# Scale and epsilon of the pooled softmax on ScalarE, and a weight queue that runs fourteen blocks ahead

## The chip, the cores and the metric

The kernel runs on one core of a Trainium2 chip. The metric is the device time of one execution in microseconds (us). Engines: PE (TensorE), DVE (VectorE), ACT (ScalarE), POOL (GpSimd) and SP, which here only issues DMAs, in order.

## What is computed

The reference, cut to what matters (batch 8, 8 heads, 576 positions, 64 elements a head):

```python
q_d, k_d, v_d = means over groups of 4 positions          # 144 pooled positions
s = scale * q_d @ k_d.T;  s = s - max(s);  a = exp(s);  a = a / (sum(a) + 1e-9)
out_up = repeat(a @ v_d, 4)
s = where(|i - j| < 4, scale * q @ k.T, -1e9)              # local attention
out_local = softmax(s, with the same 1e-9) @ v
x = (out_up + out_local) as 4608 rows of 512
h = x @ w_in                                               # 512 -> 2048
out = (h * clip(h + 3, 0, 6) / 6) @ w_out                  # 2048 -> 512
```

## The kernel before, in words

**Attention units.** A unit is one batch and a pair of heads: 8 x 4 = 32 units. Each has local scores (L570) and pooled scores (L399 or L413), two softmaxes, and the products with V (L610 local, L533 or L544 pooled). For the pooled scores, three columns of 144 in PSUM, DVE takes the maximum (L437, `top`), DVE multiplies it by -1/128 (L428, `down`), ACT does three exponentials with that as bias and with the sum as second output (L433, `weigh`), POOL adds 1e-9 to the three sums (L449, `plus`), DVE takes the reciprocal (L452) and DVE or POOL multiplies (L455, `norm`). The first two batches (8 units) transpose their weights on PE (`alone`, L464 and L593, copied out of PSUM by L119 on ACT or L121 on DVE); the other 24 units send them through DRAM and back (L477, L485, L490 pooled; L504, L511 local) and transpose on DVE (L499, L518). In those 24 the pooled scores lie in two banks: two columns in one, the third behind local scores in another; `top` and `weigh` are each called twice.

**Matrix products.** After attention the rows go in chunks through GEMM1 (L865, 16 blocks `f` of `w_in`), an activation (L871 on ACT, L875 on DVE, L879 on ACT, L883 on DVE or POOL) and GEMM2 (L915, 16 blocks of `w_out`). Chunk 0 has 512 rows. PE mixes the units of later batches with the GEMMs of the chunk that runs. In GEMM names, `h` is GEMM1's PSUM tile, `o` (and one `a`) those of GEMM2; `a` tiles otherwise belong to attention, and there are three `a` banks.

**Weights.** 32 blocks of 512 KB come as 64-bit words and are converted: L172 or L176 and L190 on ACT, L181 and L185 on DVE, L195 (high part) on ACT, L199 (low part) on DVE or POOL. The block order is i0 to i3, i4, o0, i5, o1, i6, o2, i7, o3, i8, o4 and so on (i of `w_in`, o of `w_out`). The first `GATE` = 10 loads wait only for the first inputs (and, where they use a place that early attention still holds, for that). Block n from 10 on waits until the high part of block n - 10 has been made. Beside this gate, every DMA that SP issues waits for the one eight before it.

**Order.** A planner written in the kernel (`Plan`, with costs given in each `op` call) runs through a model of the five engines and writes the instructions out in the order that comes of it. So a changed cost or dependency shifts the order of everything behind it. Engines then run their own lists in order, held only by semaphores.

## Time and profile before

| | us |
|---|---|
| median of 3 runs | 963.71 (962.75 to 965.15) |
| the profiled execution, own time | 966.26 |
| its span, first to last instruction | 964.5 |
| PE busy | 936.4 |
| DVE, ACT, POOL busy | 591.5, 343.2, 287.9 |

The profile is one execution. Its page gives busy time by engine, the chain of work that ended last, and groups of like instructions by line of the kernel; the trace can be asked for waits, stretches and single instructions. A busy PE is not PE at its peak, since its clock can be granted at half.

### The profile page before, as it was taken

How to read it: one execution, taken by the hardware profiler on the slowest of the kernel's cores; microseconds unless marked ns; L12 is line 12 of the kernel's file. 1: busy time of each engine (PE TensorE's matmuls, PEld its weight loads, DVE VectorE, ACT ScalarE, POOL GpSimd, SP SyncE). 2: the span in 40 equal slices, each digit the busy share in tenths (PEclk: the TensorE clock that was granted, in tenths of full speed). 3: DMA queues.
4: the chain of work that ended last, by engine and by line, in shares of the span. 5: the costliest groups of instructions: out<-in, count | busy, mean ns of one | idle time of the engine just before them, and what ended most of it. 6: DMA issues, size and time to landing. Idle time of an engine off the chain costs nothing.

```text
span 964.5 us, 19717 instructions
## 1 busy us (share of the span) xinstructions
PE 936.4 (97%) x7503; PEld 810.5 (84%) x7503; DVE 591.5 (61%) x1131; ACT 343.2 (36%) x805; POOL 287.9 (30%) x385
## 2 busy tenths in 40 slices
PE   8879998999999999999999999999999999999996
PEld 5558777888889788888988988888988988998995
DVE  7989787577766667657556566646645663223322
ACT  4878652334223223323323322323322322322321
POOL 5842445154535334224123223223303210000000
PEclk9979998999999999999999999999999999999999
DMA  7996525356664563545514554554424420100101
GB/s 215 251 240 210 115 80 101 87 106 128 130 133 101 108 129 76 117 79 109 118 30 83 117 101 96 121 109 80 105 47 98 95 60 1 34 1 1 34 1 33
DMA packets 311374, 93.52 MB, mean 97 GB/s; under 512 B 251376, under 2 KB 297328, under 8 KB 311280
## 3 DMA queue, kind: packets, MB, share of 16 engines
q1 hardware_dynamic: 311280, 92.27, 43.3%
q8 instruction: 59, 0.97, 0.4%
q14 instruction: 35, 0.29, 0.1%
HBM read 69.60 MB, written 22.61 MB: 96 GB/s over the span
## 4 chain that ended last, share of the span: by engine, by line
PE 79%; SPq 6%; DVE 4%; DMA 4%; POOL 3%; issue 2%; ACT 1%; DVEq 0%; POOLq 0%; ACTq 0%
PE h L865 35%; PE o L915 35%; PE a L610 2%; SPq L300 2%; PE a L570 1%; SPq L485 1%; PE a L915 1%; DMA arena<-in_k_dram 1%; PE a L413 1%; SPq L490 1%; PE a L533 1%; DMA rawo<-in_w_out_dram 1%; DMA arena<-pl 1%; DMA arena<-pd 1%; SPq L511 1%
## 5 line engine op out<-in xcount | busy, mean ns | idle before, releaser
L915 PE MATMUL o<-wo,rounded 128*128 128x512 f32 x1680 | 432.0, 398 | 2.7 <-ACT wo L195 1.3
L865 PE MATMUL h<-rounded,wi 128*128 128x384 f32 (+2 forms) x2240 | 432.8, 337 | 0.9 <-DVE arena L875 0.8
L865 PEld LDWEIGHTS h<-rounded,wi 128*128 128x128 f32 x2240 | 390.7, 189 | 23.7 <-issue 1.8
L915 PEld LDWEIGHTS o<-wo,rounded 128*128 128x128 f32 x1680 | 310.4, 189 | 64.0 <-issue 3.8
L875 DVE SCALAR_TENSOR_TENSOR arena<-arena,h 128x384 f32<-128x384 f32 (+2 forms) x192 | 104.3, 544 | 175.0 <-ACT arena L871 174.6
L871 ACT ACTIVATE arena<-h 128x384 f32<-128x384 f32 (+2 forms) x192 | 94.5, 492 | 313.8 <-PE h L865 281.9
L879 ACT CAST rounded<-arena 128x384 fp32r<-128x384 f32 (+2 forms) x192 | 98.4, 513 | 135.8 <-DVE arena L875 96.5
L883 POOL TENSOR_TENSOR rounded<-arena,rounded 128x384 fp32r<-128x384 f32 (+2 forms) x55 | 60.3, 1098 | 250.7 <-PE o L915 118.7
L883 DVE TENSOR_TENSOR rounded<-arena,rounded 128x384 fp32r<-128x384 f32 (+2 forms) x137 | 77.9, 571 | 87.4 <-PE o L915 61.0
L433 ACT ACTIVATE arena<-a,arena 128x144 f32<-128x144 f32 x84 | 31.2, 378 | 94.8 <-DVE arena L428 80.7
L455 POOL TENSOR_TENSOR arena<-arena 128x640 f32<-128x640 f32 (+1 forms) x38 | 41.8, 1111 | 17.1 <-DVE arena L452 15.5
L307 DVE STREAM_TRANSPOSE arena<-arena 128x576 f32<-128x576 f32 x56 | 42.6, 765 | 3.2 <-DMA arena<-in_k_dram 1.9
L366 DVE TENSOR_REDUCE arena<-arena 128x128 f32<-128x512 f32 (+2 forms) x34 | 36.5, 1073 | 4.8 <-PE a L533 4.3
L792 POOL TENSOR_TENSOR rounded<-arena,rounded 128x768 fp32r<-128x768 f32 (+2 forms) x9 | 12.4, 1396 | 86.7 <-DVE rounded L121 86.7
L440 POOL TENSOR_TENSOR arena<-arena 128x640 f32<-128x640 f32 x23 | 29.0, 1262 | 27.9 <-DVE arena L437 16.2
L499 DVE STREAM_TRANSPOSE arena<-arena 128x384 f32<-128x384 f32 (+1 forms) x48 | 22.0, 466 | 24.9 <-DMA arena<-pd 24.4
L518 DVE STREAM_TRANSPOSE arena<-arena 128x640 f32<-128x640 f32 x24 | 20.3, 844 | 21.5 <-DMA arena<-pl 21.4
L449 POOL TENSOR_SCALAR arena<-arena 128x10 f32<-128x10 f32 (+1 forms) x60 | 16.1, 268 | 51.1 <-ACT arena L433 41.5
L610 PEld LDWEIGHTS a<-arena 64*64 64x64 f32 x1140 | 21.0, 137 | 12.1 <-issue 3.6
L320 POOL TENSOR_TENSOR arena<-arena 128x144 f32<-128x144 f32 x24 | 11.1, 463 | 64.6 <-PE a L413 22.8
L570 PE MATMUL a<-arena 64*64 64x64 f32 x1220 | 29.4, 224 | 0.0
L322 POOL TENSOR_TENSOR arena<-arena 128x144 f32<-128x144 f32 x48 | 28.3, 589 | 3.8
(184 smaller groups left out, 836.4 us busy)
## 6 DMA issues: line engine op xcount, KB each, us to landing
rawi<-in_w_in_dram SPq DMA_DIRECT2D x16, 512.0 KB
rawo<-in_w_out_dram SPq DMA_DIRECT2D x16, 512.0 KB
arena<-in_q_dram SPq DMA_DIRECT2D x112, 72.0 KB
arena<-in_k_dram SPq DMA_DIRECT2D x112, 72.0 KB
pl<-arena SPq DMA_DIRECT2D x24, 320.0 KB
arena<-pl SPq DMA_DIRECT2D x96, 80.0 KB
arena<-in_v_dram SPq DMA_DIRECT2D x28, 256.0 KB
out_dram<-arena SPq DMA_DIRECT2D x96, 72.0 KB
```

Source lines behind the costliest of these rows:

```text
L307: nc.vector.transpose(out=qk[kind], in_=st["raw", kind].rearrange("p j i -> p (j i)"))
L366: eng.tensor_reduce(out=vd, in_=raw.rearrange("p r e -> p e r"), op=ALU.add, axis=AX.X)
L433: nc.scalar.activation(p[:, j], x[:, j], AF.Exp, bias=m[:, j:j + 1], scale=1.0 / 128.0, accum_out=s[:, j:j + 1])
L455: eng.tensor_tensor(x, x, s.unsqueeze(2).broadcast_to(list(x.shape)), op=ALU.mult)
L570: nc.tensor.matmul(st["ps", g][half:half + WIN, jj * D:jj * D + WIN], qk_of("q")[hs, k_first:k_first + WIN], qk_of("k")[hs, k_first:k_firs ...
L610: nc.tensor.matmul(st["px"][g][h * D:(h + 1) * D, at + lo:at + hi], st["v"][ks, jj, h * D:(h + 1) * D], st["pt"][ks, jj, half + lo:half + ...
L865: nc.tensor.matmul(st["ps"], win[f][:, wt, kk * P:(kk + 1) * P], xs[part][:, kk], start=(kk == 0 and i == 0), stop=(kk == NK - 1 and i == ...
L871: nc.scalar.activation(st["t"], st["ps"], AF.Relu, bias=3.0)
L875: nc.vector.scalar_tensor_tensor(out=t, in0=t, scalar=6.0, in1=st["ps"], op0=ALU.min, op1=ALU.mult)
L879: nc.scalar.copy(st["gh"], st["t"])
L883: eng.tensor_tensor(st["gl"], st["t"], st["gh"].bitcast(F32), op=ALU.subtract)
L915: nc.tensor.matmul(otile[n, m], gt[:, ms], wout[f][:, wt], start=(f == 0 and i == 0), stop=(f == NF - 1 and i == 2),)
```

## The change

The multiplication by -1/128 (`down`) goes from DVE to ACT, and the addition of 1e-9 to the pooled sums from POOL to ACT; both stand in `weigh`, around the exponentials. In the 24 later units each of the two `weigh` calls now waits for its own maximum only, where both waited for both. The local softmax keeps its POOL addition, with a planner's cost of 0.35 for 0.15. `GATE` goes from 10 to 14. Both versions hold the same matrix products; the changed one has five fewer of the 512-column products (35 to 30) that only keep PE busy before the first GEMM.

```diff
         def down(m):
-            nc.vector.tensor_scalar(m, m, -1.0 / 128.0, None, op0=ALU.mult)
+            nc.scalar.activation(m, m, AF.Copy, scale=-1.0 / 128.0)
 
         def weigh(x, p, m, s):
+            down(m)
             for j in range(x.shape[1]):
                 nc.scalar.activation(
                     p[:, j], x[:, j], AF.Exp, bias=m[:, j:j + 1], scale=1.0 / 128.0, accum_out=s[:, j:j + 1])
+            nc.scalar.activation(s, s, AF.Copy, bias=1e-9)
...
         if alone:
-            def top_d():
-                top(rows_d(), st["md"])
-                down(st["md"])
-
-            a = op("DVE", 0.68, top_d, [sd])
-            sums_d = [op("ACT", 1.74, lambda: weigh(rows_d(), st["pd"], st["md"], st["sd"]), [a], free=[bk])]
+            a = op("DVE", 0.6, lambda: top(rows_d(), st["md"]), [sd])
+            sums_d = [op("ACT", 2.2, lambda: weigh(rows_d(), st["pd"], st["md"], st["sd"]), [a], free=[bk])]
         else:
             def top_d(i):
                 x, _, m, _ = rows_d4(i)
                 top(x, m)
-                if i:
-                    down(st["md"])
 
             a, sums_d = [], []
             for i in range(2):
-                a.append(op("DVE", 0.45 - 0.07 * i, partial(top_d, i), [sd] + a))
+                a.append(op("DVE", 0.45 - 0.15 * i, partial(top_d, i), [sd]))
             for i in range(2):
-                sums_d.append(op("ACT", 1.16 - 0.58 * i, lambda i=i: weigh(*rows_d4(i)), a, free=[(bk, bks[1])[i]]))
-        a = op("POOL", 0.15, lambda: plus(st["sd"]), sums_d)
-        a = op("DVE", 0.18, lambda: recip(st["sd"]), [a])
+                sums_d.append(op("ACT", 1.62 - 0.58 * i, lambda i=i: weigh(*rows_d4(i)), [a[i]], free=[(bk, bks[1])[i]]))
+        a = op("DVE", 0.18, lambda: recip(st["sd"]), sums_d)
...
-        a = op("POOL", 0.15, lambda: plus(st["s"]), [a])
+        a = op("POOL", 0.35, lambda: plus(st["s"]), [a])
...
-PRE, GATE = 4, 10
+PRE, GATE = 4, 14
```

In the changed file lines stand up to five lower or higher; its L860, L866, L870, L874, L878, L910 are the GEMM lines L865, L871, L875, L879, L883, L915 of before, and L439, L586, L520, L629 are L437, L584, L518, L627. The DVE line L428 is an ACT line now.

**The start, SP's list.** Before, ahead of batch 1's second load of queries and keys (L300); `rawi` and `rawo` are weight blocks, here i4, o2, i5, and i6 at the end:

```order
L161 DMA rawi_520<-in_w_in_dram 128x1024
L161 DMA rawo_540<-in_w_out_dram 128x1024
L161 DMA rawi_548<-in_w_in_dram 128x1024
L300 DMA arena<-in_q_dram 32x18x32 x4
L300 DMA arena<-in_k_dram 32x18x32 x4
L340 DMA arena<-in_v_dram 64x4x128
L344 DMA arena<-in_v_dram 64x128
L161 DMA rawi_751<-in_w_in_dram 128x1024
```

And now (579 is o3, 784 is i6, 791 is o4):

```order
L161 DMA rawi_531<-in_w_in_dram 128x1024
L161 DMA rawo_541<-in_w_out_dram 128x1024
L161 DMA rawi_570<-in_w_in_dram 128x1024
L161 DMA rawo_579<-in_w_out_dram 128x1024
L300 DMA arena<-in_q_dram 32x18x32 x4
L340 DMA arena<-in_v_dram 64x4x128
L344 DMA arena<-in_v_dram 64x128
L300 DMA arena<-in_k_dram 32x18x32 x4
L161 DMA rawi_784<-in_w_in_dram 128x1024
L161 DMA rawo_791<-in_w_out_dram 128x1024
```

Block o3 moved ahead of those loads, and o4 behind i6; the keys moved behind the values.

**The same place, ACT's list.** Before, from the wait for i6 (751) to the copy out of PSUM that stood on ACT:

```order
L172 ACTIVATE o_860<-rawi_751 128x512
L871 ACTIVATE arena<-h_834 128x512
L879 CAST rounded<-arena 128x512
L190 ACTIVATE rawi_751<-rawi_751 128x512
L879 CAST rounded<-arena 128x512
L119 COPY arena<-a_879 16x3x2x48
```

Now, from the wait for i6 (784) to the second copy (`a_895`) that the first batch-1 product with pooled V needs:

```order
L172 ACTIVATE o_855<-rawi_784 128x512
L866 ACTIVATE arena<-h_830 128x512
L190 ACTIVATE rawi_784<-rawi_784 128x512
L176 ACTIVATE rawo_791<-rawo_791 128x512
L195 CAST wi_878<-o_811 128x512
L874 CAST rounded<-arena 128x512
L866 ACTIVATE arena<-h_857 128x512
L119 COPY arena<-a_890 128x3x2x48
L195 CAST wi_901<-early 128x512
L119 COPY arena<-a_895 16x3x2x48
```

The one copy on ACT stood five instructions behind the wait, and DVE made the other; now both stand on ACT, the later one nine instructions behind the wait.

**The end of chunk 0, DVE's list.** Before, around the second step (L185) of o14 (`rawo_1520`); `a_1858` and `a_1868` come from one unit's transposes and products with V on PE:

```order
L875 SCALAR_TENSOR_TENSOR arena<-arena,h_1794 128x512
L181 SCALAR_TENSOR_TENSOR arena<-rawo_1520 128x512
L307 STREAM_TRANSPOSE arena<-arena 128x576
L316 TENSOR_REDUCE arena<-arena 128x144
L121 COPY arena<-a_1858 128x256
L185 SCALAR_TENSOR_TENSOR arena<-rawo_1520,arena 128x512
L627 TENSOR_TENSOR arena<-a_1868,arena 128x288
```

And now (o14 is `rawo_1631`, o15 `rawo_1636`; `h_1774` and `h_1867` are GEMM1's last two blocks, f = 14 and 15):

```order
L870 SCALAR_TENSOR_TENSOR arena<-arena,h_1774 128x512
L181 SCALAR_TENSOR_TENSOR arena<-rawo_1631 128x512
L181 SCALAR_TENSOR_TENSOR arena<-rawo_1636 128x512
L185 SCALAR_TENSOR_TENSOR arena<-rawo_1631,arena 128x512
L878 TENSOR_TENSOR rounded<-arena,rounded 128x512
L121 CAST rounded<-arena 128x2x192
L121 CAST rounded<-arena 128x2x64
L870 SCALAR_TENSOR_TENSOR arena<-arena,h_1867 128x512
```

The copy out of PE's transposes no longer stands ahead of o14's second step, and that step moved ahead of the gate of f = 15.

**A unit in the middle, DVE's list.** Before, the eighth of the 24 units (a_3755 to a_3757 are its three banks of scores):

```order
L518 STREAM_TRANSPOSE arena<-arena 128x640
L584 TENSOR_TENSOR arena<-a_3755,mask 128x5x64
L584 TENSOR_TENSOR arena<-a_3756,mask 128x5x64
L437 TENSOR_REDUCE arena<-a_3757 128x2
L437 TENSOR_REDUCE arena<-arena 128x10
L437 TENSOR_REDUCE arena<-a_3756 128x1
L428 TENSOR_SCALAR arena<-arena 128x3
```

And now:

```order
L520 STREAM_TRANSPOSE arena<-arena 128x640
L870 SCALAR_TENSOR_TENSOR arena<-arena,h_3751 128x384
L307 STREAM_TRANSPOSE arena<-arena 128x576
L316 TENSOR_REDUCE arena<-arena 128x144
L586 TENSOR_TENSOR arena<-a_3779,mask 128x5x64
L586 TENSOR_TENSOR arena<-a_3780,mask 128x5x64
L439 TENSOR_REDUCE arena<-a_3781 128x2
L439 TENSOR_REDUCE arena<-arena 128x10
L439 TENSOR_REDUCE arena<-a_3780 128x1
```

The scaling is gone from DVE, and three instructions of other work moved between the transpose and the masks. On PE, the products with V of the unit before stand behind nine GEMM2, twelve GEMM1 and nine GEMM2 products after these scores before, and behind nine and twelve now.

## Rows read from the trace of the kernel before

**Rows 1.** The page's first part: busy us (share) and instructions of an engine.

```profile
PE 936.4 (97%) x7503; PEld 810.5 (84%) x7503; DVE 591.5 (61%) x1131; ACT 343.2 (36%) x805; POOL 287.9 (30%) x385
```

**Rows 2.** Stretches: length, busy of PE, PEld, DVE, ACT, POOL; clock; DMA share; GB/s.

```profile
44.00:68.00 24.00, 16.68 (x193) 11.64 (x187) 21.34 (x40) 19.65 (x43) 13.68 (x17) 0.85 0.86 208
...
156.00:168.00 12.00, 9.55 (x76) 7.80 (x75) 8.28 (x14) 2.06 (x4) 4.68 (x4) 0.72 0.62 123
...
319.00:334.00 15.00, 13.54 (x147) 10.91 (x147) 11.50 (x23) 4.32 (x13) 5.60 (x8) 0.89 0.52 96
334.00:950.00 616.00, 614.95 (x4568) 547.99 (x4567) 336.30 (x637) 183.35 (x430) 136.66 (x179) 1.00 0.35 73
```

**Rows 3.** PE's waits: for whom, us in total, times, longest.

```profile
PE o L915 <- ACT wo L195: 1.3, 1, 1.3
PE o L915 <- POOL wo L199: 0.8, 1, 0.8
```

**Rows 4.** Timeline, PE, 53 to 68 us: start, us, what [idle before].

```profile
53.58 0.39 PE L865 MATMUL h<-rounded,wi 128*128 128x512 f32 x1
...
59.06 1.42 PE L544 MATMUL a<-arena 128*64 128x144 f32 x8 [2.74 <-DVE arena L121]
...
62.12 1.49 PE L610 MATMUL a<-arena 64*64 64x60 f32 x38 [0.38 <-ACT arena L119]
...
67.18 1.06 PE L570 MATMUL a<-arena 64*64 64x64 f32 x40
68.17 0.79 PE L865 MATMUL h<-rounded,wi 128*128 128x512 f32 x1
```

**Rows 5.** Timeline, ACT, 56 to 57 us.

```profile
56.18 0.63 ACT L172 ACTIVATE o<-rawi 128x512 f32<-128x512 f32 x1 [2.70 <-DMA rawi<-in_w_in_dram]
56.74 0.58 ACT L871 ACTIVATE arena<-h 128x512 f32<-128x512 f32 x1
```

**Rows 6.** Timeline, SP, 44 to 51 us: loads as issued.

```profile
44.33 4.96 SPq L300 DMA_DIRECT2D arena<-in_k_dram  x4
...
50.63 0.58 SPq L161 DMA_DIRECT2D rawi<-in_w_in_dram  x1
```

**Rows 7.** The chain that ended last, 157 to 161 us: start, us, what.

```profile
157.17 1.41 DVE arena L185
...
158.60 0.63 ACT wo L195
...
159.29 1.28 POOL wo L199
```

**Rows 8.** Line L428, its instructions: ns least/median/most.

```profile
L428 DVE TENSOR_SCALAR arena<-arena x30: 169/675/1172, 13.4 to 775.7; 128x3 f32<-128x3 f32 x30
```

**Rows 9.** Timeline, POOL, 28 to 31 us.

```profile
28.81 2.11 POOL L455 TENSOR_TENSOR early<-early,arena 128x640 f32<-128x640 f32 x2
```

**Rows 10.** Timeline, DVE, 29 to 31 us.

```profile
29.69 1.26 DVE L428 TENSOR_SCALAR early<-early 128x3 f32<-128x3 f32 x1
```

**Rows 11.** Groups by line: count, busy us, mean ns, idle before.

```profile
L549 ACT ACTIVATE arena<-a 128x144 f32<-128x144 f32 x28 | 8.2, 293 | 11.1 <-PE a L533 9.5 <-PE a L544 1.6
...
L433 ACT ACTIVATION_READ_ACCUMULATOR arena<-a,arena 128x1 f32 x84 | 16.8, 200 | 0.0
```

**Rows 12.** Timeline, PE, 319 to 329 us.

```profile
319.39 0.58 PE L413 MATMUL a<-arena 64*64 64x144 f32 x10
...
328.85 0.74 PE L610 MATMUL a<-arena 64*64 64x57 f32 x34 [1.46 <-ACT arena L433]
```

**Rows 13.** Timeline, DVE, 323 to 328 us.

```profile
325.36 0.44 DVE L437 TENSOR_REDUCE arena<-a 128x2 f32<-128x288 f32 x1
...
326.77 1.11 DVE L428 TENSOR_SCALAR arena<-arena 128x3 f32<-128x3 f32 x1
```

**Rows 14.** Timeline, ACT, 328 us.

```profile
327.96 0.38 ACT L433 ACTIVATE arena<-a,arena 128x144 f32<-128x144 f32 x1 [5.50 <-DVE arena L428]
```

**Rows 15.** The chain that ended last, 397 us: nine products of GEMM2.

```profile
397.25 2.26 PE o L915 x9
```

## Prediction

> **What bounds the kernel now.** I began with the page's first part: PE is busy for 936.4 us of a span of 964.5, DVE for 591.5 [rows 1]. So the time is PE's products, plus about 28 us in which PE stands, plus what a halved clock takes. A change that touches only DVE, ACT and POOL can win or lose at those two places alone. The second view, busy time by stretch, says where they are [rows 2]. From 334 to 950 us PE works 614.95 of 616 us at full clock: nothing is to be won there, only lost. In 44 to 68 PE works 16.68 of 24 us at a mean granted clock of 0.85, in 156 to 168 it works 9.55 of 12 at 0.72, in 319 to 334 it works 13.54 of 15 at 0.89. The clock has two levels (1.2 and 2.4 GHz); a mean of 0.85 over 24 us is 7.2 us at the lower one, which costs half of that, 3.6 us. In the same way the second place costs 3.4 us and the third 1.65. Each time PE had just stood.
>
> The waits of PE, the timelines and the chain of waits tell what it stood for.
>
> *The start.* The third block of GEMM1 ends at 53.58 + 0.39 = 53.97 us, the fourth (f = 3) begins only at 68.17 [rows 4]. Between them stand attention products, of which the first with pooled V waits 2.74 us for a copy by DVE; DVE is busy for 21.34 and ACT for 19.65 of these 24 us. ACT stood 2.70 us for weight block i6, until 56.18 [rows 5]. SP issued that load at 50.63, behind batch 1's keys and values, which it had begun to issue before 44.33 [rows 6].
>
> *The end of chunk 0.* DVE's second step of o14 begins at 157.17 (in the order ahead, a copy of PE's transposes stands ahead of it), then come ACT at 158.60 and POOL at 159.29 [rows 7]. GEMM2 waits 1.3 us for ACT's part and 0.8 for POOL's [rows 3].
>
> *In the middle.* At 327 to 329 us PE waits 1.46 us for exponentials, 328.85 - 319.39 = 9.46 us after it began that unit's pooled scores [rows 12]. The chain there is `top` 325.36, `down` at 326.77, which takes 1.11 us, exponentials at 327.96 [rows 13, 14].
>
> **The change part by part. 1. The scaling leaves DVE.** The 32 instructions L428 take 169 ns at the least, 675 in the median, 1172 at the most [rows 8] (30 on that row and two with another name, as in [rows 10]); 32 x 0.675 = 21.6 us of DVE. The long ones are not arithmetic on 128x3 numbers. One began at 29.69 and ran 1.26 us, to 30.95; POOL's multiplication beside it ended at 28.81 + 2.11 = 30.92 [rows 9, 10]. I read this as DVE held until POOL lets go.
>
> DVE has 279.7 us to spare in 616 (336.30 busy), so from 334 us on these microseconds are off the path: 0. At the start, where DVE is nearly full, eight units pass and the stalls lie on the path; a gain from them is inside the bounds of point 3.
>
> **2. ACT gains 112 small instructions**: two in each of 8 early units, four in each of 24 later ones. The trace has no such copy. The nearest rows are ACT's 128x1 read of an accumulator, 200 ns, and a 128x144 activation, 293 ns [rows 11]. So one costs 0.2 to 0.29 us, and all 22 to 33 us of ACT. ACT is busy for 183.35 of 616 us in the middle [rows 2]; there they lie on no path except the unit's own chain. In that chain `top`, the wait, `down` (1.41 + 1.11 us from 325.36 to 327.88 at the eighth unit, [rows 13]) become `top` (0.44) and one ACT copy (0.2 to 0.29): the first exponentials can start about 1.8 us earlier after the first maximum. POOL's addition goes to ACT as well, which shortens the other side of the chain by a handover; it is not waited for by PE in any row here: 0. At the start 16 of the copies stand in ACT's list, where it is busy 82%: 16 x 0.25 = 4.0 us over all 8 units; if four of them fall ahead of the wait that ends last there, 1 us, which is within the bounds of point 3.
>
> **3. GATE 14, at the start.** o3 now stands ahead of batch 1's loads on SP, and o4 behind i6; 14 blocks are loaded before a conversion is asked for. What is queued behind: SP's queue puts o3's 524 kB ahead of batch 1's keys and i6. At the stretch's 208 GB/s [rows 2] that is 2.5 us, so i6 lands at 56.2 (no change, if the transfers had room) to 58.7; or at 53.5, if its issue goes forward by as much. On ACT both copies that the first batch-1 product with pooled V needs stand behind the wait for i6, the later one behind nine other instructions. ACT's instructions begin 0.56 us apart [rows 5]; with the two smaller copies the ten take, as an estimate, 4.8 us. Then come the L544 and L593 products, 1.4 us at full clock (L544 took 1.42 at half, [rows 4]), and 0.4 for handovers: f = 3 starts 6.6 us after i6 lands. With 56.2 that is 62.8, against 68.17: 5.4 us earlier. But L610 (1.49) and L570 (1.06), which stood ahead of f = 3, now follow it: 2.5 us of the work is only moved. The net is -2.9; with 53.5 it is -5.6, with 58.7 it is -0.4. f = 3's own weight can also be ready only late; its low part is made some 7 us of DVE's work earlier in the new list, so it is not what comes last there. If the nine instructions on ACT take half as long again (2.4 us more) behind a late i6, the sum is +2.0. I take -2.5, nearest to the landing seen, less a little for ACT's copies.
>
> **4. The end of chunk 0.** The second step of o14 no longer stands behind the copy that waited for PE, and three pieces of GEMM work (a piece is 2.26 us or more, [rows 15]) stand on PE between that unit's products with V and o14. The chain of 1.41, 0.63 and 1.28 us on DVE, ACT and POOL [rows 7], 3.3 us, fits under 6.8. So the waits of 1.3 and 0.8 us and the 3.4 us of halved clock, in all 5.5, can go. But ACT's part of o14 now stands behind the activation of f = 15, and if this wait only moves, nothing goes. The bounds are -5.8 (with the 0.3 us of waits below those rows) and 0; I take -4, since two of three engines in the chain lose the wait for PE.
>
> **5. The middle.** Each `weigh` now waits only for its own maximum, so exponentials can start some 1.8 us earlier. In the new order, though, PE's products with V stand mostly one piece closer behind the next scores: nine GEMM2 products are 2.26 us [rows 15], and at the eighth unit of 24 nine of them are gone from in between, as in about 15 of the units. So PE needs the exponentials 2.26 us earlier, against the 1.8 that they gain: 0.46 us less cover in those units. Before, the stop of 1.46 us with 1.65 us of clock behind it (3.1 us) was the one of its kind with such a price. It may go (-3.2 us) or be joined by others; three other DVE instructions that moved ahead of the eighth unit's masks make a stop there no less likely. Bounds -3.1 and +8 (two or three such stops more); I take +1. Five fewer filler products cost nothing: they run when PE has nothing else.
>
> **The sum**, against the profiled execution's own time of 966.26: -2.5 (start) - 4 (end of chunk 0) + 1 (middle) = -5.5, so 960.8. The median of the runs before is 963.71, 2.55 below that execution: **958.2 us** as a median, 0.6% faster. What 3 runs can tell from no change is about 0.3%, 2.9 us.
>
> **The rivals.**
>
> *A, the forecast*: start and chunk 0's end gain 4 to 10 us and the middle takes back about 1: 954 to 960.8. Chance 0.40.
>
> *B, the middle also gains.* The stop at 327 us goes (-3.1 in place of +1), and chunk 0's end gains all of its 5.8: with the start's -2.5 that is -11.4, 952.3; with -5.6 there it is -14.5, 949.2. For it: [rows 13] show `down` in the chain in full. Against it: the order spends the 1.8 us by moving products with V closer. 949 to 953, 0.12.
>
> *C, the change doesn't do what it says.* The loads come earlier but i6, ACT's list or o14's chain holds PE for as long: the gains of points 3 and 4 shrink to 0 to 3 us, 961 to 966. For it: i6 still has to land, and ACT and DVE are 82 and 89% busy in that stretch [rows 2]. 0.20.
>
> *D, slower.* One mechanism: products with V one piece closer behind the scores. The masks' and maxima's path on DVE and the exponentials on ACT take as long as the pieces left between (two pieces of 2.26 to 3 us), so that PE waits in several units. Each stop of the [rows 12] kind costs 1.46 plus 1.65 of clock, 3.1 us; with five such the sum of points 3 and 4, -6.5, becomes +9, that is 963.71 + 9 = 973, with four 969.6. It decides where exponentials start later than about 5 us after the unit's first product of scores, which the eighth unit (8.57 us, 327.96 - 319.39) already did before. For it: DVE held by POOL at any place. Against it: 614.95 of 616 us of PE at work from 334 on, so most units had cover to give. 967 to 973, 0.20.
>
> *E, ACT is the wrong engine.* At the start ACT is on the path to f = 3. Sixteen more activations at 0.293 us [rows 11] are 4.7 us; if all of it lies ahead of f = 3, it takes back nearly all of the sum: 963.71 - 5.5 + 4.7 = 962.9. Against it: half of the eight units are batch 0's, whose copies stand ahead of the wait for i6, in which ACT stood 2.70 us anyway [rows 5]. 0.08.
>
> The Trainium skill ("ScalarE: Activation LUTs", § Rules for kernel authors) bids use VectorE, not ScalarE, for additions and multiplications, which speaks against this change. By its figure for an activation with immediates (§ What ACT_TABLE_LOAD costs, 186 ns and 0.833 ns an element) one copy would be about 189 ns and 112 of them 21 us, an estimate from that page. No run here shows that copy; by the page's figure the sum stays the same, since ACT's additions lie beside other work in it.
>
> **How the numbers follow.** A (0.40) and B (0.12) are faster by over 0.3%: 0.52. C and E (0.28) lie within 0.3%. D, 0.20, is slower. The range leaves out the lowest part of B, below 950 (0.03), and the worse part of D, above 968.5 (0.15): it is 950 to 968.5.
>
> **What would show it.** Point 1 and 2: no L428 on DVE; the new copies on ACT at 0.2 to 0.29 us each; DVE's busy time down by some 15 to 22 us, ACT's up by 22 to 33. Point 3: ACT's wait for i6 ends at 53.5 to 58.7, f = 3 starts near 62.8, PE's wait for the copies before L544 shrinks. Point 4: no wait of GEMM2 for `wo` from ACT or POOL near 157 us, and a clock of 1.00 behind it. Point 5: PE's waits in L610 for ACT number two or fewer and the stretch 334 to 950 stays at 1 us of idle time or little more. The prediction is wrong if f = 3 starts at 68 us or later, if the wait at the end of chunk 0 comes back under another name, or if the waits for exponentials come to more than 6 us with the clock behind them.

## The result and the profile after

The changed kernel took 957.7 us in the median of 5 runs (956.95 to 958.59), the kernel before 965.15 (962.75 to 971.36, 5 runs). The ratio is 0.9901, with a 95% interval of 0.9875 to 0.9928: about 1% faster. (The quotient of the two medians is 0.9923, near the upper end of that interval, so the change is worth some 7 to 12 us.) The profiled execution of after took 956.95 us, that of before 966.26; the span fell from 964.5 to 954.8.

The page's first part, as in [rows 1]: busy us (share) and instructions.

```profile
PE 931.0 (98%) x7498; PEld 805.4 (84%) x7498; DVE 573.0 (60%) x1096; ACT 368.2 (39%) x915; POOL 279.3 (29%) x371
```

DVE lost 18.5 us, ACT gained 25.0, POOL lost 8.6. The same stretches as [rows 2] (length, busy of PE, PEld, DVE, ACT, POOL, clock, DMA share, GB/s), and the sum for 334 to 940 us:

```profile
44.00:68.00 24.00, 18.19 (x152) 13.07 (x152) 21.25 (x40) 20.10 (x45) 10.04 (x14) 0.93 0.94 302
...
156.00:168.00 12.00, 11.89 (x75) 10.51 (x74) 7.14 (x12) 3.80 (x10) 2.53 (x3) 1.00 0.45 86
...
319.00:334.00 15.00, 15.00 (x121) 12.96 (x119) 9.84 (x20) 5.95 (x18) 6.85 (x10) 1.00 0.51 115
```

```profile
sum 606.00, PE 606.00 PEld 540.80 DVE 320.48 ACT 196.00 POOL 126.39; mean PE 606.00 PEld 540.80 DVE 320.48 ACT 196.00 POOL 126.39
```

All three places of [rows 2] are better: 1.5 us more of PE at work and clock 0.93 for 0.85 at the start, 2.3 us more and full clock at the end of chunk 0, no stop between 319 and 334. (After is 3 to 6 us ahead in its work by then, so a stretch doesn't hold the same products in the two kernels.) From 334 us PE never stands (in 334 to 940 before it worked 604.95 of 606). PE's waits now, as in [rows 3]:

```profile
PE h L860 <- ACT wi L195: 3.7, 2, 2.9
...
PE a L546 <- ACT arena L119: 2.1, 2, 1.7
PE o L910 <- POOL rounded L878: 0.9, 1, 0.9
```

No wait for exponentials is left among them.

To see where the time went, I laid PE's records of two traces beside each other: each product is counted with its line's usual spacing in the trace of before, and the table says how much earlier (-) or later than in the profiled execution of before PE had the same amount of work behind it. The columns are the points that PE reached at 103, 173, 321, 390 and 696 us before. All kernels of the experiments stand in it, to be read with them.

| kernel | 103 | 173 | 321 | 390 | 696 |
|---|---|---|---|---|---|
| after | -2.8 | -6.2 | -5.9 | -8.2 | -9.8 |
| order | -1.1 | -4.3 | -0.1 | -1.8 | -3.4 |
| instr | 0.0 | -1.2 | -1.2 | -2.1 | -3.4 |
| down_only | +3.1 | +0.4 | +2.5 | +2.4 | +1.8 |
| gate14 | +0.5 | +1.2 | +1.8 | +0.5 | +1.6 |
| soft10 | +1.3 | +2.0 | +7.2 | +4.0 | +2.3 |
| gate12 | +3.1 | +1.8 | +13.7 | +11.5 | +10.1 |
| o14_swap | +2.5 | +0.5 | +2.4 | +2.6 | +4.3 |
| o14_all | +1.0 | -1.5 | +1.0 | +1.2 | +2.8 |
| instr_o14 | +2.2 | -0.6 | 0.0 | +1.5 | +0.4 |
| i6_first | -2.5 | -5.7 | -5.5 | -7.8 | -9.4 |
| i6_o4 | -3.2 | -6.5 | -6.2 | -7.6 | -9.3 |
| twice | -1.5 | -4.9 | -4.1 | -5.9 | -7.5 |

So the change brought 2.8 us by the time that the first GEMM blocks ran, 3.4 more at the end of chunk 0, and 3.6 more behind that, 2.3 of it at the stop of 327 us. Two cautions belong beside it. First, o14_swap, o14_all and before have the same lists of instructions up to 150 us, and still stand at +2.5, +1.0 and 0.0 in the first column. One trace against another tells the start only to some 3 us; the verdicts below therefore go by the ratios of many runs, and the profile says where. What does hold is that the five kernels with after's order (or one or two places off it) stand at -1.1 to -3.2 there, and the six with the lists of before at 0.0 to +3.1.

Second, the granted clock differs between executions even behind the same stops. `instr` and `down_only` have both waits for o14 of [rows 3] (1.25 and 0.85 us in either), and yet come out 1.2 and 2.7 us better than before between 103 and 173. The same stretch behind these stops in `instr`, then, 3 us later, in `down_only`; before had a clock of 0.72 there [rows 2]:

```profile
156.00:168.00 12.00, 9.55 (x84) 7.98 (x83) 8.68 (x15) 2.65 (x6) 4.62 (x4) 0.86 0.63 124
```

```profile
159.00:171.00 12.00, 9.54 (x95) 8.18 (x94) 9.03 (x17) 3.65 (x8) 4.82 (x4) 1.00 0.62 121
```

So the half clock behind the same two stops cost 3.4, 1.7 and 0 us in these three executions. The 3.4 us of after's gain at the end of chunk 0 are against an execution that paid the most.

### The profile page after: what moved, and what is told of

Same layout as the page of the kernel before. It is cut to its first block, busy times and chain, and to the rows that moved or that the text cites. A ratio compares the mean times of both kernels' runs of the same rounds, so it can differ in the third digit from the quotient of the medians.

```text
span 954.8 us, 19793 instructions
## 1 busy us (share of the span) xinstructions
PE 931.0 (98%) x7498; PEld 805.4 (84%) x7498; DVE 573.0 (60%) x1096; ACT 368.2 (39%) x915; POOL 279.3 (29%) x371
## 4 chain that ended last, share of the span: by engine, by line
PE 88%; DMA 3%; SPq 2%; DVE 2%; POOL 2%; ACT 1%; issue 1%; DVEq 0%; POOLq 0%
PE h L860 40%; PE o L910 40%; PE a L612 2%; PE a L572 2%; PE a L413 1%; PE a L535 1%; PE a L910 1%; DMA early<-in_v_dram 1%; DMA rawo<-in_w_out_dram 1%; DMA rawi<-in_w_in_dram 1%; SPq L300 1%; POOL early L368 1%; SPq L252 0%; SPq L487 0%; DVE arena L870 0%
## 5 line engine op out<-in xcount | busy, mean ns | idle before, releaser
L860 PE MATMUL h<-rounded,wi 128*128 128x384 f32 (+2 forms) x2240 | 433.2, 336 | 5.0 <-ACT wi L195 3.7
L910 PE MATMUL o<-wo,rounded 128*128 128x512 f32 x1680 | 429.1, 396 | 1.0 <-POOL rounded L878 0.9
L860 PEld LDWEIGHTS h<-rounded,wi 128*128 128x128 f32 x2240 | 389.8, 188 | 28.5 <-ACT wi L195 4.5
L910 PEld LDWEIGHTS o<-wo,rounded 128*128 128x128 f32 x1680 | 308.1, 188 | 62.4 <-issue 4.6
L870 DVE SCALAR_TENSOR_TENSOR arena<-arena,h 128x384 f32<-128x384 f32 (+2 forms) x192 | 105.0, 547 | 175.0 <-ACT arena L866 174.5
L866 ACT ACTIVATE arena<-h 128x384 f32<-128x384 f32 (+2 forms) x192 | 94.1, 490 | 285.5 <-PE h L860 279.9
L874 ACT CAST rounded<-arena 128x384 fp32r<-128x384 f32 (+2 forms) x192 | 98.4, 513 | 145.9 <-DVE arena L870 107.8
L878 DVE TENSOR_TENSOR rounded<-arena,rounded 128x384 fp32r<-128x384 f32 (+2 forms) x154 | 87.1, 567 | 103.0 <-PE o L910 77.0
L878 POOL TENSOR_TENSOR rounded<-arena,rounded 128x384 fp32r<-128x384 f32 (+2 forms) x38 | 42.8, 1126 | 213.2 <-PE o L910 137.9
L787 POOL TENSOR_TENSOR rounded<-arena,rounded 128x768 fp32r<-128x768 f32 (+2 forms) x6 | 8.8, 1472 | 94.9 <-DVE rounded L121 82.3
L428 ACT ACTIVATE arena<-arena 128x2 f32<-128x2 f32 (+2 forms) x54 | 10.6, 197 | 63.4 <-DVE arena L439 63.4
L520 DVE STREAM_TRANSPOSE arena<-arena 128x640 f32<-128x640 f32 x24 | 20.2, 841 | 22.8 <-DMA arena<-pl 22.6
L457 DVE TENSOR_TENSOR arena<-arena 128x432 f32<-128x432 f32 (+1 forms) x38 | 31.5, 830 | 1.0
L368 POOL TENSOR_TENSOR arena<-arena 128x256 f32<-128x256 f32 (+2 forms) x37 | 29.2, 789 | 4.6 <-DMA arena<-in_v_dram 3.3
L439 DVE TENSOR_REDUCE arena<-a 128x2 f32<-128x288 f32 (+3 forms) x63 | 25.1, 406 | 3.9 <-PE a L572 2.0
```

Source lines behind the costliest of these rows:

```text
L368: eng.tensor_tensor(raw[:, 0:2], raw[:, 0:2], raw[:, 2:4], op=ALU.add)
L457: eng.tensor_tensor(x, x, s.unsqueeze(2).broadcast_to(list(x.shape)), op=ALU.mult)
L860: nc.tensor.matmul(st["ps"], win[f][:, wt, kk * P:(kk + 1) * P], xs[part][:, kk], start=(kk == 0 and i == 0), stop=(kk == NK - 1 and i == ...
L866: nc.scalar.activation(st["t"], st["ps"], AF.Relu, bias=3.0)
L870: nc.vector.scalar_tensor_tensor(out=t, in0=t, scalar=6.0, in1=st["ps"], op0=ALU.min, op1=ALU.mult)
L874: nc.scalar.copy(st["gh"], st["t"])
```

## The experiments

Each ratio is to runs of the kernel before on the same chip. The kernel before had medians of 967.87, 970.15 and 968.49 us in the three sets.

**GATE alone, and the softmax edit alone.**

```diff
--- before
-PRE, GATE = 4, 10
+PRE, GATE = 4, 14
```

> The kernel before with GATE 14 alone; the pooled softmax stays as it was. Theory (weights ahead are worth the start and the end of chunk 0): between the two kernels PE's products stand 2.8 us earlier where chunk 0 runs and another 3.5 us earlier behind its end, so 965.15 - 6.3 = 958.9 us; no wait of GEMM2 for weights near 157 us, but a stop of PE for exponentials remains somewhere between 200 and 340 us. Rival (the order that the planner finds counts, not the weights): any time from 960 to 968, with stops of PE at other places. Rival (the gain needs both edits): 963 to 966.

Measured: 1.0056 (1.0036 to 1.0076), slower. Its profiled execution, 967.97 us, was the fastest of its 12, so its row in the table flatters it. PE's waits:

```profile
PE a L399 <- DVE arena L627: 4.5, 1, 4.5
PE a L610 <- ACT arena L433: 2.9, 3, 1.6
...
PE o L915 <- DVE wo L199: 2.0, 1, 2.0
```

In this order the fourth block of GEMM1 starts at 70.7 us, later than the 68.17 of [rows 4], although ACT never waits for i6: PE stands 4.5 us for DVE instead. The loads that run ahead are not by themselves a gain.

```diff
--- after
-PRE, GATE = 4, 14
+PRE, GATE = 4, 10
```

> The changed kernel with GATE back at 10: the softmax edit alone. Theory: only the middle gains, 965.15 - 3.6 = 961.5 us; ACT's copies 0.2 us each; the wait of GEMM2 for weights at the end of chunk 0 stays or comes at another of its blocks. Rival (the softmax edit brings the most): below 959.5. Rival (nothing of its own): 964 to 967.

Measured: 1.0026 (1.0014 to 1.0039), a little slower. The planner found an order with other stops:

```profile
PE a L595 <- DVE arena L457: 3.9, 1, 3.9
PE a L466 <- POOL early L457: 3.3, 1, 3.3
PE h L860 <- POOL rounded L787: 3.2, 2, 2.7
```

Neither edit alone makes the kernel faster, and together they give 0.9901. So the gain can't be shared out between the two edits; what has to be separated is the instructions from the order.

**The order of before with the instructions of after, and the reverse.** In `instr` every list is as before, but the 32 scalings and the 32 pooled additions stand in ACT's list inside `weigh`:

```diff
--- before
-                if i:
-                    down(st["md"])
...
-        a = op("POOL", 0.15, lambda: plus(st["sd"]), sums_d)
+        a = op("POOL", 0.15, lambda: None, sums_d)
```

(with `down` and `weigh` of the changed kernel). In `order` every list is as after, but the scaling stands on DVE behind each maximum and the addition on POOL:

```diff
--- after
                 top(x, m)
+                down(m)
...
-        a = op("DVE", 0.18, lambda: recip(st["sd"]), sums_d)
+        a = op("DVE", 0.18, lambda: (plus(st["sd"]), recip(st["sd"])), sums_d)
```

(with `down` and `weigh` of the kernel before; each `weigh` still waits for its own maximum only).

> The order of the kernel before on every engine, GATE 10, but with the changed kernel's instructions: the scaling and the addition stand in ACT's list inside weigh, the 32 scalings on DVE and 32 additions on POOL are gone, nothing else moves. Theory (the middle's gain is the shorter chain itself): exponentials start about 1.8 us earlier, the stop of 1.46 us at 327 us and the 1.65 us of clock behind it go: 965.15 - 3.1 = 962.0 us, down to 960.5 if the start gains from DVE's freed time as well. Rival (it was the new order that took the stops away): 964 to 966 with the stop near 327 us still there.

> The order of the changed kernel on every engine, GATE 14, but the scaling on DVE right behind each maximum (56 instructions) and the addition of 1e-9 on POOL, ahead of the reciprocal. Theory (the new order spends the 1.8 us by putting products with V a piece of 2.26 us closer behind the scores, so it needs the shorter chain): PE stops for exponentials in two to five units, each at 1 to 3 us with its clock: 957.7 + 3 to 9 = 961 to 967 us. Rival (the order alone makes the gain): 957 to 959 us and no more waits of PE than in the changed kernel.

Measured: `instr` 0.9969 (0.9952 to 0.9985), `order` 0.9949 (0.993 to 0.9968). At the eighth unit `instr` shows what the shorter chain does. PE's wait for exponentials there, 1.46 us in [rows 12], is down to 0.29, and the clock stays full:

```profile
326.52 0.74 PE L612 MATMUL a<-arena 64*64 64x57 f32 x34 [0.29 <-ACT arena L434]
```

In `order` the chain is the long one of before, and still PE waits for no exponentials anywhere. Its stops are others:

```profile
PE o L909 <- POOL rounded L877: 2.2, 1, 2.2
PE h L859 <- DVE rounded L786: 1.7, 1, 1.7
```

They stand at 201.65 and 222.65 us, where after stands for 0.94 and 0.68 us, and behind the first the clock is granted at 0.66 from 201 to 206 us (1.00 in after), which costs 1.7 us. Together that is 4.0 us, what it loses to after between 173 and 321 in the table (3.9). So both halves are real: the instructions are worth 0.3% in the old order (0.9969) and 0.5% in the new one (0.9949 to 0.9901, from different sets), the new order 0.5% with the old instructions. `order` was expected to be 3 to 9 us slower than after through waits for exponentials; it is some 5 us slower, but through other waits, so the time came as the theory had it and the mechanism did not.

**Which of the two moved instructions counts.**

```diff
--- instr
-            nc.scalar.activation(s, s, AF.Copy, bias=1e-9)
...
-        a = op("POOL", 0.15, lambda: None, sums_d)
+        a = op("POOL", 0.15, lambda: plus(st["sd"]), sums_d)
```

> As the run that kept the order of the kernel before and took the changed instructions, but only the scaling goes to ACT; the addition stays on POOL in its old place. Theory (the addition is waited for by nobody on the path): the whole of that run's gain, ratio 0.997 to the kernel before, and no stop of PE at 327 us. Rival (the POOL addition, with its handovers, held the pooled side up): 0.998 to 1.000.

Measured: 0.9971 (0.9946 to 0.9996), as `instr` within these intervals, so that no effect of the addition's place is seen. The expectation that PE has no stop at this place was missed: it waits 1.02 us at the eighth unit in the profiled execution, for 0.29 in `instr`. The ratio of 12 runs shows no loss from it.

**Does ACT's extra work lie on the path?**

```diff
--- after
-            nc.scalar.activation(m, m, AF.Copy, scale=-1.0 / 128.0)
+            nc.scalar.activation(m, m, AF.Copy, scale=-1.0 / 16.0)
+            nc.scalar.activation(m, m, AF.Copy, scale=1.0 / 8.0)
...
-            nc.scalar.activation(s, s, AF.Copy, bias=1e-9)
+            nc.scalar.activation(s, s, AF.Copy, bias=0.5e-9)
+            nc.scalar.activation(s, s, AF.Copy, bias=0.5e-9)
```

> The changed kernel in its own order with each of the 112 small copies on ACT made as two of the same kind (a scaling in two factors, 1e-9 in two halves), so 112 more instructions of 0.2 us, 22 us more of ACT. Theory (point 2: they lie on no path that sets the end, apart from the start's few): the same time as the changed kernel within 1 us, ratio to the kernel before 0.990 to 0.991. Rival E (ACT is on the path at the start, 16 of them there, or the units' chains are): 2 us or more above the changed kernel, 0.992 or more.

Measured: 0.9887 (0.9856 to 0.9917), not slower than after by the ratios. The page's first part of this kernel:

```profile
PE 933.0 (97%) x7498; PEld 806.7 (84%) x7498; DVE 571.8 (60%) x1096; ACT 387.8 (41%) x1027; POOL 278.5 (29%) x371
```

112 more instructions and 19.6 us more of ACT, and the 2 us or more of the rival lie outside the interval. That they cost 1 us can't be excluded.

**The end of chunk 0.** First one exchange in DVE's list of before (`d` is the second step of o14, `p` the copy ahead of it), then the whole conversion of o14:

```diff
--- before, o14_swap
         self.order = order
+        d = MARKS["o", 14][1]
+        p = [o for o in order if o.eng == "DVE"]
+        p = p[p.index(d) - 1]
+        order.remove(d)
+        order.insert(order.index(p), d)
```

> The kernel before, with one pair of neighbours exchanged in DVE's list and nothing else moved: the second step of block o14 stands ahead of the copy out of PE's transposes, not behind it. Theory of the prediction's point 4: the step begins some 1.5 to 2 us earlier, GEMM2 no longer waits 1.3 and 0.8 us for o14's parts and the clock behind stays at full: up to 5.5 us less, ratio to the kernel before 0.9943 to 0.996. Rival (the wait only moves: the copy is now 0.6 us later and PE stands for it, or ACT's and POOL's parts come last anyway): 0.999 to 1.001.

Measured: 0.9983 (0.9958 to 1.0008), which can't be told from no change. The timelines of POOL, DVE and PE of this kernel show why:

```profile
157.97 2.96 POOL L884 TENSOR_TENSOR rounded<-arena,rounded 128x512 fp32r<-128x512 f32 x2
160.89 1.27 POOL L199 TENSOR_TENSOR wo<-arena,wo 128x512 fp32r<-128x512 f32 x1
```

```profile
158.26 1.53 DVE L185 SCALAR_TENSOR_TENSOR arena<-rawo,arena 128x512 int32<-128x512 int32 x1
```

```profile
162.21 3.17 PE L916 MATMUL o<-wo,rounded 128*128 128x512 f32 x7 [0.80 <-POOL wo L199]
```

The step took 1.53 us beside POOL's two products, and o14's low part stood in POOL's list behind those two. The 1.3 us wait is gone, the 0.8 us wait is not.

```diff
--- before, o14_all
         self.order = order
+        ahead(d, 3)
+        ahead(hi, 1)
+        ahead(lo, 2)
```

(`ahead` moves an operation so many places forward in its engine's list: the second step on DVE right behind the first, the high part on ACT ahead of a copy that waits for PE, the low part on POOL ahead of two products for GEMM2.)

> The kernel before, with the whole conversion of block o14 moved forward and nothing else: its second step on DVE three places earlier (right behind the first), the high part on ACT one place (ahead of a copy that waits for PE), the low part on POOL ahead of two products for GEMM2. The single exchange on DVE left POOL's 0.8 us wait, since POOL ran 2.9 us of products ahead of the low part. Theory (o14's readiness sets the end of chunk 0): the block is ready by about 157.5 us, the waits of 1.3 and 0.8 us and the 3.4 us of halved clock behind them go: ratio to the kernel before 0.994 to 0.996. Rival (POOL's products that are now 1.3 us later are what GEMM2 waits for, or the clock halves anyway): 0.998 to 1.001.

> The order of the kernel before with the changed instructions (which alone gave 0.997) and the whole conversion of o14 moved forward as in the run beside it. Theory (the two are separate causes and add): 0.997 - 0.005 = 0.992 to the kernel before, so most of the whole change's 0.990 without GATE 14 and without the new order. Rival (only the first counts): 0.996 to 0.998.

Measured: `o14_all` 0.9987 (0.9968 to 1.0006), `instr_o14` 0.9939 (0.9919 to 0.9958). PE's stops behind 150 us in `o14_all`:

```profile
158.08 1.16 PE L611 MATMUL a<-arena 64*64 64x60 f32 x40 [0.35 <-ACT arena L119]
163.75 2.30 PE L866 MATMUL h<-rounded,wi 128*128 128x256 f32 x17 [0.49 <-POOL rounded L793]
166.59 0.73 PE L916 MATMUL o<-wo,rounded 128*128 128x512 f32 x2 [0.23 <-DVE wo L199]
167.89 1.69 PE L866 MATMUL h<-rounded,wi 128*128 128x256 f32 x12 [0.57 <-DVE arena L876]
```

No wait for o14 is left, but three new ones of 0.49, 0.23 and 0.57 us stand behind, for what now runs later on POOL and DVE. In the table the kernel gains 2.5 us between 103 and 173; against before the ratio is 1.3 us, not clear of zero; on top of the changed instructions it is 2.9 us (0.9969 to 0.9939). So the conversion of o14 is worth some 1 to 3 us: the waits that go (1.25 and 0.85 us) come back for the most part (1.29 us in three), within 10 us.

What remains is the clock, by all runs and not by one trace. Worked out as one less the mean granted clock, times the span, the half clock costs 10.2 us in the 26 runs of before of this set and 8.0 in the 12 of `o14_all`; it costs 10.5 in `instr` (its own set) and 7.8 in `instr_o14`. That is 2 to 3 us less in either pair, an estimate, where the theory had 3.4 from one execution.

**The start.** In after, i6's load five places earlier on SP; then in addition the first step of o4 behind the two copies on ACT (`ld` is the load of i6, moved ahead of o3's; `first` is the first step of o4, moved behind `a_895`'s copy):

```diff
--- after, i6_first
         self.order = order
+        ld = MARKS["i", 6][0]
+        p = [o for o in order if o.eng == "SP"]
+        p = p[p.index(ld) - 4]
+        order.remove(ld)
+        order.insert(order.index(p), ld)
--- i6_o4, in addition
+        p = [o for o in order if o.eng == "ACT"]
+        p = p[p.index(first) + 6]
+        order.remove(first)
+        order.insert(order.index(p) + 1, first)
```

> The changed kernel with one load moved in SP's list and nothing else: weight block i6 is loaded ahead of o3 and of batch 1's second loads, five places earlier. Theory of the prediction's point 3 (the fourth block of GEMM1 starts 6 us after i6 lands, held by ACT's list): i6 is there before 50 us, ACT's wait of 3.07 us for it at 57.23 is gone, the fourth block starts at 60 us where it started at 63.0, and the time falls by 2 to 3 us: ratio to the kernel before 0.987 to 0.988, against 0.990. Rival (batch 1's loads are late by a block's 2.5 us and its units then hold PE): 0.990 to 0.994. Rival (something else is late next at the same moment): 0.990.

Measured: 0.9894 (0.9861 to 0.9927), as after. ACT's timeline in this kernel:

```profile
54.22 0.66 ACT L172 ACTIVATE o<-rawi 128x512 f32<-128x512 f32 x1
56.35 0.60 ACT L867 ACTIVATE arena<-h 128x512 f32<-128x512 f32 x1 [1.48 <-PE h L861]
...
59.32 0.70 ACT L176 ACTIVATE rawo<-rawo 128x512 f32<-128x512 f32 x1 [1.81 <-DMA rawo<-in_w_out_dram]
```

i6 no longer holds ACT, but a product of PE and then o4's load do, and the copies come at 61.38 and 62.17 us, half a microsecond later than in after.

> The changed kernel with i6's load five places earlier, as before, and the first step of o4 on ACT moved behind the two copies of PE's transposes: with i6 early, ACT stood 1.81 us for o4's load instead, until 59.32. Theory (ACT's list behind a load holds the fourth block of GEMM1): the copies come about 1.5 to 2 us earlier than at 60.87 and 61.67, the fourth block starts at 61 to 61.5 us in place of 63.0 to 63.5: 1.5 to 2 us less than the changed kernel, ratio 0.988. Rival (the block is moved but the work behind it waits for DVE, which is full): as the changed kernel, 0.990.

Measured: 0.9888 (0.9862 to 0.9914), median 957.24: as after within the intervals. PE's timeline:

```profile
50.83 0.80 PE L861 MATMUL h<-rounded,wi 128*128 128x512 f32 x1 [3.58 <-ACT wi L195]
...
60.87 0.47 PE L547 MATMUL a<-arena 128*64 128x144 f32 x4 [0.16 <-ACT arena L119]
61.67 0.46 PE L547 MATMUL a<-arena 16*64 16x144 f32 x4 [0.33 <-ACT arena L119]
...
62.58 0.48 PE L861 MATMUL h<-rounded,wi 128*128 128x512 f32 x1
```

The wait for the copies is down from 1.74 us to 0.16, since the copies come 0.45 us earlier than in after (60.41 and 61.23 us), yet the fourth block starts only 0.4 us earlier: PE itself comes later. The 3.58 us are not the reason: the second block starts at 50.83 us here and at 50.87 in after. But this and the third block together end at 59.37 us, in after at 58.24, because the granted clock (the third number from the end) is lower here. After, then `i6_o4`:

```profile
50.00:58.00 8.00, 7.13 (x24) 5.55 (x25) 5.69 (x11) 4.93 (x10) 3.65 (x4) 0.79 0.76 209
```

```profile
50.00:58.00 8.00, 7.17 (x19) 5.65 (x20) 6.47 (x13) 6.28 (x13) 3.63 (x4) 0.58 0.57 114
```

Without that 1.1 us the fourth block would come at some 61.5 us, an estimate and the upper end of what the theory expected. So one profiled execution neither bears the theory out nor refutes it, and the ratio can't tell 0.988 from 0.990.

**Another gate.**

```diff
--- after
-PRE, GATE = 4, 14
+PRE, GATE = 4, 12
```

> The changed kernel with GATE 12 in place of 14. With the same softmax edit, 10 gave 1.0026 and 14 0.990 of the kernel before. Theory by now (it is the order that the planner happens to find, not how far the loads run ahead): anywhere from 0.989 to 1.004, with stops of PE at other places than with 10 or 14. Rival (the gain grows with the gate): 0.996, halfway, with GEMM2's wait for weights at chunk 0's end half as long as with 10.

Measured: 1.0077 (1.005 to 1.0104), slower than with 10, far slower than with 14, and outside the 0.989 to 1.004 of the theory. Two of PE's stops:

```profile
151.55 0.50 PE L860 MATMUL h<-rounded,wi 128*128 128x512 f32 x1 [2.04 <-ACT wi L195]
...
228.26 3.55 PE L860 MATMUL h<-rounded,wi 128*128 128x384 f32 x11 [5.52 <-DVE rounded L787]
```

With the same softmax edit, gates of 10, 12 and 14 give 1.0026, 1.0077 and 0.9901. That is no trend in the gate. That the planner's order decides is the reading that is left, argued from where PE stops and not tested by itself. The 5.52 us stop is for a split of a chunk's rows on DVE (L787), which no edit touches.

## Why the prediction held, point by point

The time was forecast at 958.2 us, and the median is 957.7. That it came so close is luck: the base was too low and the gain too small, by nearly as much. The direction, the range and the two places of the gain were right; one term of the sum had the wrong sign.

*The base.* The forecast went from a median of 963.71. Later sets of the kernel before have medians of 965 to 970 us, so the base was 1.4 us or more too low. And the change is worth 7.5 us by the two medians, 9.5 by the ratio, where the sum said 5.5.

*Point 1, the scaling leaves DVE.* Right in DVE's time (18.5 us less, 15 to 22 forecast). Its reading of the long ones holds throughout the trace of before: of the 32 scalings 11 took 0.17 us, and each of the 21 longer ones ended 0.02 or 0.03 us behind an instruction of POOL. `instr` and `down_only` give 0.3% in the old order, but they can't tell the freed DVE time from the shorter chain of point 5. At the start, `instr` still has its fourth block at 67.3 us (68.17 before), so there the freed DVE time alone moved little.

*Point 2, the ACT instructions.* Right: 112 of 0.19 to 0.20 us, at the low end of the bounds. Groups by line, count, busy us, mean ns, idle before:

```profile
L436 ACT ACTIVATE arena<-arena 128x2 f32<-128x2 f32 x24 | 4.9, 204 | 0.8
L428 ACT ACTIVATE arena<-arena 128x2 f32<-128x2 f32 x24 | 4.9, 204 | 62.2 <-DVE arena L439 62.2
...
L428 ACT ACTIVATE arena<-arena 128x1 f32<-128x1 f32 x24 | 4.6, 190 | 0.4 <-DVE arena L439 0.4
```

ACT's busy time rose by 25.0 us, within the 22 to 33 forecast. `twice` puts 112 more beside them without a cost that can be seen; rival E, with its 4.7 us, falls. The page "ScalarE: Activation LUTs" of the Trainium skill (§ What ACT_TABLE_LOAD costs) gives 186 ns and 0.833 ns an element for this form, and the trace agrees within 10%. Its rule to use VectorE for additions and multiplications (§ Rules for kernel authors) is one about speed per element. Here the scaling took 169 ns on DVE at the least, less than on ACT, but 675 in the median [rows 8], and there the rule misleads.

*Point 3, the start.* Right in size; its reason is not shown. ACT's wait for i6 ended at 57.23 us, within the 56.2 to 58.7 forecast, and the fourth block started at 63.0, where 62.8 was named:

```profile
57.23 0.62 ACT L172 ACTIVATE o<-rawi 128x512 f32<-128x512 f32 x1 [3.07 <-DMA rawi<-in_w_in_dram]
```

```profile
50.87 0.66 PE L860 MATMUL h<-rounded,wi 128*128 128x512 f32 x1 [2.94 <-ACT wi L195]
...
61.31 0.47 PE L546 MATMUL a<-arena 128*64 128x144 f32 x4 [1.74 <-ACT arena L119]
62.10 0.46 PE L546 MATMUL a<-arena 16*64 16x144 f32 x4 [0.33 <-ACT arena L119]
63.02 0.47 PE L860 MATMUL h<-rounded,wi 128*128 128x512 f32 x1
```

The net was put at -2.5, and PE stands 2.8 us earlier at 103 us. But the sum lacks a term: PE now waits 2.94 us for the second block's weight, at 50.87 us. Before, that block began at 48.00 without a wait, since ACT made that weight's high part at 45.94 and now does at 50.20; the third block ended at 53.97 and now ends at 58.24. So the fourth block comes 5 us earlier behind a third that comes 4 us later, and that the net agrees is in part luck. Whether the chain "i6, nine instructions on ACT, copies, fourth block" holds the block is open: with i6 early, ACT's list waits for PE and for o4's load instead, and the block starts no earlier (63.52, `i6_first`); with the list cleared too, PE comes late at a lower clock, and the block gains 0.4 us (`i6_o4`). Nor does GATE 14 cause the gain alone: `gate14` has that block at 70.7 us. Two slips in the prediction's working change nothing: 56.2 less 2.5 is 53.7, not 53.5, and the stop at 327 us stands once at 3.2 and otherwise at 3.1.

*Point 4, the end of chunk 0.* Right for o14: PE's chain here is

```profile
154.47 0.61 DVE arena L185
...
155.10 0.63 ACT wo L195
...
155.80 1.30 POOL wo L199
...
157.15 2.11 PE o L910 x8
```

and PE takes up the last of o14's products 0.05 us behind POOL's last write, without a stop; the clock stays full. Against -4, PE gains 3.4 us there. But more than half of the 2.1 us of waits is back under another name, which the prediction named as a sign of being wrong: GEMM1's last block waits for its weight, which it did not before.

```profile
150.34 0.50 PE L860 MATMUL h<-rounded,wi 128*128 128x512 f32 x1 [0.72 <-ACT wi L195]
...
151.53 0.73 PE L860 MATMUL h<-rounded,wi 128*128 128x512 f32 x2 [0.46 <-DVE wi L199]
```

So most of this gain is the half clock, 3.4 us in this execution of before and less in others. The cause was too narrow as well: putting the step ahead of the copy moved nothing that can be measured, and bringing the whole block forward is worth 1 to 3 us, since POOL's and DVE's other work then comes late. The new order has that work elsewhere; that this makes the difference is not shown.

*Point 5, the middle.* The step that failed: +1 was put, and PE gained 3.6 us. The table has medians over the 24 units, in us behind a unit's first product of the scores, worked out from the records of the traces. At the eighth unit PE went on at 328.85 us [rows 12], right behind the second exponential, whose sum was read by 328.80; the last column is the time from that read to the first product with V.

| kernel | first exponential | first product with V | cover |
|---|---|---|---|
| before | 4.8 | 7.7 | 1.8 |
| instr | 3.5 | 7.7 | 3.4 |
| order | 3.3 | 6.3 | 1.8 |
| after | 3.0 | 6.3 | 1.9 |

The exponentials gain the 1.8 us forecast, and in 11 units (some 15 were put) the products with V come 2.1 us closer, so that their cover shrinks by 0.4 us, where 0.46 was forecast. What failed is the price: less cover is no stop while some is left. The smallest cover in after is 0.5 us and no unit stands, while at the eighth unit of before it was 1.7 us short. So the stop of 3.1 us went and none joined it. `order` has the same covers with the scaling still on DVE, and `instr` takes most of that stop away in the old order: either half of the change is enough, or nearly so, at this place.

At the eighth unit (timelines of PE and ACT):

```profile
316.60 0.58 PE L413 MATMUL a<-arena 64*64 64x144 f32 x10
...
322.19 0.81 PE L612 MATMUL a<-arena 64*64 64x60 f32 x40
```

```profile
320.12 0.20 ACT L428 ACTIVATE arena<-arena 128x2 f32<-128x2 f32 x1 [3.14 <-DVE arena L439]
320.36 0.38 ACT L434 ACTIVATE arena<-a,arena 128x144 f32<-128x144 f32 x1
```

The first exponential comes 3.8 us behind the scores, where it came 8.57 us behind before [rows 12, 14], and PE doesn't wait. `order`, with the long chain, has no stop at this unit either.

*The rivals.* What happened is A in its time (954 to 960.8) with the middle of B, whose 949 to 953 it did not reach: the end of chunk 0 gave 3.4 us, not 5.8. D did not happen in its mechanism: no kernel with after's order waited for exponentials for more than 0.6 us in all. But the outcome on that side was nearer than 0.20 says: of four combinations of gate and softmax edit, three are slower than before, by 0.3 to 0.8%, through stops at places that have to do with neither edit.

What stays open: why the profiled start of kernels with the same lists differs by up to 2.5 us (the granted clock up to 103 us, 0.95 in before, 0.93 in `o14_swap` and 0.97 in `o14_all`, accounts for it only in part), which of the order's many moves brings the start's gain, and how much of after's 1% a planner that found another order with the same two edits would keep. A GATE above 14 was not tried. No run was clearly faster than after; `i6_o4`, at 957.24 us, comes out level with it.

## What to carry to other kernels

When a planner writes the order, split a change into its instructions and its order: run the new instructions in the old order and the old ones in the new order, and only then say which edit pays. Here the two halves were worth 0.3 to 0.5% each, while each edit by itself was slower. A stop at the end of a chain of three engines was not worth its whole length here: clear one engine's place in the list, and look in the lists of the other two before counting the gain. And what a half clock cost in one execution is not its price in all: behind the same stops it was 3.4, 1.7 and 0 us. Before half a microsecond is read out of two traces, compare their granted clocks in that stretch.

## What the runs showed of the hardware

DVE's step with two inputs, L185 at 128x512, took 0.68 us in after (154.38 us), at a time when POOL waited, and 1.53 us beside POOL's two products of 2.96 us (`o14_swap`); in the kernel before it took 1.48 us beside two such products (its 1.41 us in the chain of [rows 7]). The Trainium skill's "GPSIMD Engine Reference" (§ 8 Key points) says that the two engines share SBUF interfaces and contend where DVE has two SBUF inputs, and this agrees. It need not be DVE that waits: at 148.5 us in after two such DVE steps took 0.68 and 0.72 us, and POOL's two instructions on 32x64 numbers beside them (L373) took 1.28 and 1.25, where 0.44 is usual. A step with one input can wait as well: the scalings on DVE, 128x3 numbers, took 0.17 us or else lasted until POOL's instruction ended (21 of 32).

ACT scales 128x2 numbers in 204 ns, and 112 more such instructions cost the kernel nothing that could be measured, in a list that is busy for 39% of the time.

Behind the same two stops of 1.25 and 0.85 us at the end of chunk 0, PE's mean granted clock over 12 us was 0.72, 0.86 and 1.00 in three executions (before, `instr`, `down_only`).

The same kernel differs from run to run by up to 1.2% (962.53 to 974.5 us for the kernel before in one set), and after and its three neighbours (`twice`, `i6_first`, `i6_o4`) by 0.2 to 0.5%. That is more than the effect of most single moves; two of them, `o14_swap` and `o14_all`, stay undecided. Part of it is the clock: in the 23 runs of that set it was granted at 0.984 to 0.995 in the mean, and the longer runs mostly had the lower (correlation of time and time lost to the clock: 0.73).
